# A slot's score steps in two visits to the row halves of the PE array, weight pieces behind the softmax, and another spread of the first groups

## The chip, the core and the metric

The kernel runs on one core of a Trainium2 chip. PE is TensorE, DVE is VectorE, ACT is ScalarE, POOL is GpSimd, SP issues the transfers; PEld is PE's loading of weights. The metric is the device time of one launch in microseconds, the median of three runs.

## The reference

Block-causal attention feeds a gated feed-forward with a spatial mix. Eight batches, eight heads, 576 positions, 64 dimensions a head, float32:

```python
scores = (q @ k.T) / 8                     # 576 x 576 per head, rows see blocks of 64 up to their own
attn   = softmax(scores)                   # with + 1e-9 in the divisor
x      = (attn @ v), heads side by side    # 576 x 512 per batch
h      = gelu(x @ w_in)                    # 576 x 1024, halves u and v
v_n    = (v - mean) / sqrt(var + 1e-6) * g_ln
v_s    = w_sg @ v_n + b_sg                 # over the 576 positions
out    = x + (u * v_s) @ w_out
```

`w_in` and `w_out` arrive as doubles.

## The kernel before

**Slots.** The attention of a pair of heads is a slot: 32 slots, four to a batch, n from 0. In slot n the kernel finishes pair n (transposes of the probabilities, products with the values, normalising) and makes scores and softmax of pair n+1. The rows of scores come in five tiles, 0 with 64 rows and 1 to 4 with 128; tile i reaches to column 64 + 128 i.

**Parts of the PE array.** Three kinds of matmul follow each other in a slot. Transposes of whole blocks (`pa`, `pb`, `pc`, `pe`, written `turn0`, `turn2`, `turn1`, `turn_sums`) and the feed-forward's groups use the whole array, 128 rows by 128 columns. Scores (`s`, steps 1 to 4) and the half blocks on the diagonal (`turn2_rest`, `turn1_rest`, `turn_first`) use its row halves, 64 rows. The products with the values (`ob`, `av0`, `av2`, `av1`, `av00`) use its column halves, 64 columns, one per head.

**Softmax.** A step writes its scores to two PSUM banks, one per head. DVE's `maximum` moves them to `prob` and keeps the negated maximum `negm`; tile 4 needs step1 and step2. ACT's `exponent` follows, and its sums go to `sums`. Then the next slot transposes `prob` into `pa`, `pb`, `pc`, and ACT and DVE copy these to `pt`.

**Groups.** The feed-forward of a batch runs in the holes of later slots: `hole(k)` issues k groups, one PSUM accumulation each. Of a batch there are 5 groups v, 8 u, 8 s, 8 o, and o stands behind the next batch's u. In steady state a slot n with n%4 = 0 has the v groups and two of u, n%4 = 1 the other u groups and one o, n%4 = 2 seven o, n%4 = 3 eight s. `PLAN` says how many groups go into each hole; `FIRST` says it for slots 4 to 7, the first that have any. When the v or u groups of a batch are done, ACT runs their GELU, with a table load before and after; layer norm and splitting into high and low parts follow on DVE, ACT and POOL (`run_side`).

**PSUM.** Five banks, tag "s", serve scores, groups and `ob`; `ob` is held from `av0` to the end of the slot. Three banks, tag "p", serve the transposes in turn, so a slot's second `pb` takes the bank of its first `pa`.

**Weights.** They are loaded and split in pieces, drawn by `weight_step`. A piece of `w_in` or `w_out` (128 x 256 doubles) costs a scaling on ACT, one tensor_scalar and two scalar_tensor_tensor on DVE, a cast on ACT and a subtraction on POOL. There are 16 pieces of `w_in`, 8 of `w_out`, 5 of `w_sg` and the gains. `WS` says how many steps a slot draws, `load_share` spreads them over four places; two are drawn before slot 0.

**What sets the order.** PE issues in program order (`PIN = "P"`). The other engines are ordered by a scheduler at build time, with its own picture of time, and may pull an instruction ahead of others of the program; `tc.issue_after` names an instruction that has to be issued before.

Of the kernel before, what the change touches and what calls it, by code (L numbers as in the profile page):

```python
# [28 lines left out]
def kernel(  # L29
# [73 lines left out]
    V, A, G, SP = Pinned(nc.vector, "V"), Pinned(nc.scalar, "A"), Pinned(nc.gpsimd, "G"), Pinned(nc.sync, "S")  # L103
# [116 lines left out]
    def load_weight(src, cols, dh, dl):  # L220

        W, AHEAD = 256, 4
        parts = [(c, slice(f, f + W)) for f in range(cols.start, cols.stop, W) for c in range(NC)]
        raws = {}

        def fetch(k):
            if k < len(parts):
                c, fs = parts[k]
                raws[k] = page(src.dtype, W, "raw")
                SP.dma_start(raws[k], src[c * P : (c + 1) * P, fs])  # L230

        for k in range(AHEAD):
            fetch(k)
        for k, (c, fs) in enumerate(parts):
            args = (raws.pop(k), dh[:, c, fs], dl[:, c, fs])
            if src.dtype == F32:
                split_weight(*args)
            else:
                from_f64(*args)
            fetch(k + AHEAD)  # L240
            yield True

    def load_spatial():
        for j in range(NT - 1):
            t = page(F32, S, "w")
            SP.dma_start(t, w_sgT[j * P : (j + 1) * P, :])
            split_weight(t, ws_h[:, j, :], ws_l[:, j, :])
            yield True

        j = NT - 1  # L250
        t = page(F32, S, "w")
        for hf in (0, 1):
            SP.dma_start(t[hf * BLK : (hf + 1) * BLK, :], w_sgT[j * P : S, :])
        t2 = page(F32, S, "w")
        G.memset(t2[BLK:, :], 0.0)
        SP.dma_start(t2[BLK : BLK + 1, :], b_sg.unsqueeze(0))
        SP.dma_start(t2[96:97, :], b_sg.unsqueeze(0))
        A.copy(ws_h[:, j, :], t)
        G.tensor_tensor(
            ws_l[:BLK, j, :], t[:BLK, :], ws_h[:BLK, j, :].bitcast(F32), op=ALU.subtract  # L260
        )
        A.copy(ws_l[BLK:, j, :], t2[BLK:, :])
        V.tensor_tensor(
            ws_l[96:97, j, :], t2[96:97, :], ws_l[96:97, j, :].bitcast(F32), op=ALU.subtract
        )
        yield True

    def load_gains():
        SP.dma_start(g_bc, g_ln.unsqueeze(0).broadcast_to([P, DH]))
        t = page(F32, S, "w")  # L270
        G.memset(t[BLK:, :DH], 1.0)
        V.tensor_copy(vone[BLK:, :], t[BLK:, :DH])
        yield True

    weights = deque(
        [
            ("v", load_weight(w_in, slice(DH, DFF), wi_h, wi_l)),
            ("v", load_gains()),
            ("u0", load_weight(w_in, slice(0, DH // 2), wi_h, wi_l)),
            ("u2", load_weight(w_in, slice(DH // 2, DH), wi_h, wi_l)),  # L280
            ("s", load_spatial()),
            ("o", load_weight(w_out, slice(0, DM), wo_h, wo_l)),
        ]
    )

    def weight_step():

        while weights and next(weights[0][1], None) is None:
            weights.popleft()

    def need(part):

# [3 lines left out]

    spill = {}
    xs = {}

    class Scores:  # L300

# [32 lines left out]
        def maximum(self, a, i, lo, hi):  # L334

            r, e = slice(0, QN[i]), EXT[i]
            m = self.negm[a][r, i : i + 1]
            V.tensor_tensor_reduce(
                self.prob[a][i][r, lo:hi],
                self.where[a, i, lo],  # L340
                mask[r, MW - (hi - lo) :] if 0 < i and hi == e else mask[r, : hi - lo],
                -0.125,
                3.0e38 if lo == 0 else m,
                op0=ALU.add,
                op1=ALU.min,
                accum_out=m,
            )

        def exponent(self, a, i):
            r, e = slice(0, QN[i]), EXT[i]  # L350
            A.activation(
                self.prob[a][i][r, :e],
                self.prob[a][i][r, :e],
                AF.Exp,
                bias=self.negm[a][r, i : i + 1],
                scale=-1.0,
                accum_out=self.sm[r, i, a : a + 1],
            )
# [153 lines left out]
    def run_side(k):  # L512

        while k > 0 and side and side[0][0] != "G":
            k -= 1
            side.popleft()[1]()
# [201 lines left out]
    def hole(k=1):  # L718

        while k > 0 and work:  # L720
            try:
                next(work[0])
                k -= 1
            except StopIteration:
                work.popleft()
# [3 lines left out]
    def load_share(n, k):  # L729

        if n < len(WS):
            for _ in range(WS[n] * (k + 1) // 4 - WS[n] * k // 4):
                weight_step()

    PLAN = ["1111111", "1111111", "1111111", "1111112"]

    FIRST = ["1111111", "1111110", "0000011", "1111110"]

    def slot(n, sc):
        va = Values(n, sc)  # L740
        nx = Scores(n + 1) if n + 1 < N else None
        g = [int(x) for x in (FIRST if n // 4 == 1 else PLAN)[n % 4]]
        if n + 2 < N:
            load_qk(n + 2)
        if n + 1 < N:
            load_v(n + 1)
        va.inverse()
        va.turn0(0)
        va.turn0(1)
        hole(g[0])  # L750
        load_share(n, 0)
        run_side(2)

        if nx:
            nx.step1()
        va.av0()
        if nx:
            nx.exponents(1)
        va.turn2()
        hole(g[1])  # L760
        run_side(2)
        va.turn2_rest()
        if nx:
            nx.step2()
        load_share(n, 1)
        hole(g[2])
        if nx:
            nx.exponents(4)
        run_side(2)
        va.turn1()  # L770
        va.turn1_rest()
        va.turn_first()
        if nx:
            nx.step3()
        va.av2()
        hole(g[3])
        load_share(n, 2)
        run_side(2)
        if nx:
            nx.exponents(3, 0)  # L780
            nx.step4()
        va.av1()
        va.av00()
        va.turn_sums()
        if nx:
            nx.exponents(2)
        hole(g[4])
        va.normalise()

        wait = n // (H // 2) > 0 and n % (H // 2) < 2  # L790
        pending.append(va.split)
        if not wait:
            while pending:
                pending.popleft()()
        run_side(2)
        if n + 2 < N:
            split_qk(n + 2)
        load_share(n, 3)
        hole(g[5])
        run_gelu()  # L800
        run_side(3)
        hole(g[6])
        run_side(3)
        if n % (H // 2) == 1:
            while pending:
                pending.popleft()()
        return nx
# [75 lines left out]
```

## Time and profile before

| | us |
|---|---|
| runs, median of three (lowest, highest) | 804.05 (802.69, 805.39) |
| profiled execution | 805.21 |
| its span | 803.1 |
| PE busy in it | 774.1 (96%) |
| DVE, ACT, POOL busy | 488.6, 452.4, 273.9 |
| slots 0 to 3 | 9.5 to 82.9 |
| slots 4 to 7 | 82.9 to 172.6 |
| slots 8 to 31 | 172.6 to 733.7 |
| groups behind the last slot | 733.7 to 803.1 |

A slot's start is read off PE's order of time: the first transpose into `pa`. In that view a row has start, length, engine, line, operation, tiles and count, and in brackets the idle time before it with what ended it. Lengths of matmuls overlap, so what one costs is the distance of two starts. The views by stretch give each engine's busy time between two times, and the granted clock as a share of full speed. A line of the source is nearly always that of a helper (L88 matmul, L91 transpose, L101 all other engines), so tiles' names tell rows apart; buffer numbers are left out.

### The profile page before, as it was taken

Reading aid. Unit: us, or ns where it says so; the run is one execution under the profiler, and the core shown is the slowest. Engines: PE = TensorE matmul, PEld = TensorE weight load, DVE = VectorE, ACT = ScalarE, POOL = GpSimd, SP = SyncE. Lnnn points to the kernel's source line nnn. Section 1 sums busy time; section 2 is a strip of 40 time slices with the busy share of each in tenths; the row PEclk is TensorE's granted clock in tenths of the full one; section 3 lists DMA queues with packets and bytes.
Section 4 is the critical chain, followed back from the end, with each engine's and each line's share of the span. In section 5 each row is a group of like instructions: output and inputs, shape, how many; then the busy total and the mean of one; then the engine's idle time right before and its main releaser. Section 6 shows DMA issues by size and latency. Waiting matters only on the chain.

```text
span 803.1 us, 15777 instructions
## 1 busy us (share of the span) xinstructions
PE 774.1 (96%) x5926; PEld 642.1 (80%) x5926; DVE 488.6 (61%) x1457; ACT 452.4 (56%) x1172; POOL 273.9 (34%) x331
## 2 busy tenths in 40 slices
PE   7579998999999999999999999999999999999998
PEld 5355686888888888897888888888888978888998
DVE  6955468884865567563765648655675637743532
ACT  5846569656864368435783368642694457821600
POOL 4773235651233314350233412333143402322111
PEclk8878998999999999999999999999999999999999
DMA  7522124212041123310242120321234102320042
GB/s 235 165 75 89 60 89 139 86 61 74 31 144 52 58 75 93 130 60 1 74 133 90 60 75 20 120 87 58 75 90 134 60 1 75 104 75 30 1 118 74
DMA packets 46911, 65.66 MB, mean 82 GB/s; under 512 B 4082, under 2 KB 22514, under 8 KB 46836
## 3 DMA queue, kind: packets, MB, share of 16 engines
q1 hardware_dynamic: 46836, 64.67, 25.1%
q8 instruction: 46, 0.75, 0.4%
q14 instruction: 29, 0.24, 0.1%
HBM read 45.78 MB, written 18.87 MB: 81 GB/s over the span
## 4 chain that ended last, share of the span: by engine, by line
PE 83%; ACT 0%; DVE 0%; issue 0%
PE accs L88 15%; PE acco L88 13%; PE accv L88 12%; PE accu L88 11%; PE ob L88 10%; PE s L88 9%; PE pb L91 4%; PE pc L91 3%; PE pa L91 3%; PE pe L91 1%; PE pd L91 1%; PE pd L88 0%; ACT pt L101 0%; DVE xr L101 0%; ACT w L101 0%
## 5 line engine op out<-in xcount | busy, mean ns | idle before, releaser
L101 ACT ACTIVATE prob<-prob,negm 128x448 f32<-128x448 f32 (+4 forms) x320 | 177.5, 557 | 107.3 <-DVE negm L101 104.6
L101 POOL TENSOR_TENSOR qk_l<-qk_f,qk_h 128x576 fp32r<-128x576 f32 x62 | 89.3, 1461 | 270.3 <-PE pe L91 114.0
L101 DVE CUSTOM_DVE_ANT_0 prob<-s,mask 128x288 f32<-128x288 f32 (+2 forms) x320 | 119.2, 422 | 78.9 <-PE s L88 77.4
L88 PE MATMUL ob<-pt,v_f 128*64 128x512 f32 (+4 forms) x640 | 111.7, 455 | 2.5 <-ACT pt L101 2.5
L101 POOL TENSOR_TENSOR gl<-u,gh 128x288 fp32r<-128x288 f32 x64 | 52.0, 818 | 114.1 <-DVE gh L101 89.1
L88 PE MATMUL s<-qk_h 64*128 64x288 f32 (+1 forms) x372 | 83.2, 353 | 0.0
L88 PE MATMUL accs<-ws_h,vh 128*128 128x288 f32 x256 | 78.6, 307 | 0.0
L88 PE MATMUL accu<-xh,wi_h 128*128 128x288 f32 x256 | 78.6, 307 | 0.0
L88 PE MATMUL acco<-gh,wo_h 128*128 128x288 f32 x256 | 78.2, 305 | 0.0
L88 PE MATMUL accu<-xl,wi_h 128*128 128x288 f32 x256 | 75.5, 295 | 0.0
L88 PE MATMUL accs<-ws_h,vl 128*128 128x288 f32 x256 | 75.5, 295 | 0.0
L88 PE MATMUL accs<-ws_l,vh 128*128 128x288 f32 x256 | 75.5, 295 | 0.0
L88 PE MATMUL accu<-xh,wi_l 128*128 128x288 f32 x256 | 75.5, 295 | 0.0
L88 PE MATMUL acco<-gh,wo_l 128*128 128x288 f32 x256 | 75.4, 294 | 0.0
L88 PE MATMUL acco<-gl,wo_h 128*128 128x288 f32 x256 | 75.4, 294 | 0.0
L88 PE MATMUL s<-qk_l,qk_h 64*128 64x288 f32 (+1 forms) x372 | 70.1, 297 | 0.9 <-POOL qk_l L101 0.9
L88 PEld LDWEIGHTS ob<-pt,v_f 128*64 128x64 f32 x640 | 38.9, 139 | 38.6 <-issue 21.6
L88 PE MATMUL s<-qk_h,qk_l 64*128 64x288 f32 (+1 forms) x372 | 65.5, 297 | 1.9 <-POOL qk_l L101 1.9
L88 PE MATMUL accv<-wi_h,xh 128*128 128x512 f32 x160 | 66.1, 413 | 0.0
L101 DVE TENSOR_TENSOR u<-accs,u 128x288 f32<-128x288 f32 x64 | 29.1, 454 | 56.1 <-PE accs L88 56.1
L88 PE MATMUL accv<-wi_l,xh 128*128 128x512 f32 x160 | 63.0, 393 | 0.0
L101 DVE TENSOR_TENSOR xr<-acco,xr 128x288 f32<-128x288 f32 x64 | 29.1, 455 | 54.9 <-PE acco L88 46.3
(104 smaller groups left out, 1948.9 us busy)
## 6 DMA issues: line engine op xcount, KB each, us to landing
spill<-x SPq DMA_DIRECT2D x32, 288.0 KB, 2.1
xr<-spill SPq DMA_DIRECT2D x32, 288.0 KB, 3.1
out_T<-xr SPq DMA_DIRECT2D x32, 288.0 KB, 2.9
qk_f<-in_qT SPq DMA_DIRECT2D x31, 288.0 KB, 2.9
qk_f<-in_kT SPq DMA_DIRECT2D x31, 288.0 KB, 3.4
v_f<-in_v SPq DMA_DIRECT2D x32, 256.0 KB, 3.0
raw<-in_w_in SPq DMA_DIRECT2D x16, 256.0 KB, 4.9
raw<-in_w_out SPq DMA_DIRECT2D x8, 256.0 KB, 3.0
```

Source lines behind the costliest of these rows:

```text
L88: return pin(nc.tensor.matmul(*a, **k), "P")
L91: return pin(nc.tensor.transpose(out, in_, identity), "P")
L101: return lambda *a, **k: pin(f(*a, **k), self.letter)
```

## The change

Inside a slot, `turn2` and `turn2_rest` move up behind the first hole, and step1 and step2 follow them directly; `av0` comes after both, and the exponents of tiles 1 and 4 after it. The second hole and the third now have nothing between them but a load share and `run_side`. Step4 moves up behind step3, ahead of `av2`, and the exponents of tiles 3, 0 and 2 stand together behind `av2`. Counted on PE, the array's part changes eight times in a slot and not eleven.

`newest` keeps the latest maximum and the latest exponent that the program has issued, and `weight_step` makes everything of a piece wait in the order for both. `FIRST` has 7, 6, 4 and 4 groups in slots 4 to 7, where it had 7, 6, 2 and 6.

```diff
     def weight_step():
 
-        while weights and next(weights[0][1], None) is None:
-            weights.popleft()
+        with ExitStack() as stack:
+            for ins in newest.values():
+                stack.enter_context(tc.issue_after(ins.ins))
+            while weights and next(weights[0][1], None) is None:
+                weights.popleft()
...
-            V.tensor_tensor_reduce(
+            newest["V"] = V.tensor_tensor_reduce(
...
-            A.activation(
+            newest["A"] = A.activation(
...
-    FIRST = ["1111111", "1111110", "0000011", "1111110"]
+    FIRST = ["1111111", "1111101", "0011011", "1011010"]
...
         run_side(2)
 
+        va.turn2()
+        va.turn2_rest()
         if nx:
             nx.step1()
+            nx.step2()
         va.av0()
         if nx:
-            nx.exponents(1)
-        va.turn2()
+            nx.exponents(1, 4)
         hole(g[1])
+        load_share(n, 1)
         run_side(2)
-        va.turn2_rest()
-        if nx:
-            nx.step2()
-        load_share(n, 1)
         hole(g[2])
-        if nx:
-            nx.exponents(4)
         run_side(2)
         va.turn1()
         va.turn1_rest()
         va.turn_first()
         if nx:
             nx.step3()
+            nx.step4()
         va.av2()
+        if nx:
+            nx.exponents(3, 0, 2)
         hole(g[3])
         load_share(n, 2)
         run_side(2)
-        if nx:
-            nx.exponents(3, 0)
-            nx.step4()
         va.av1()
         va.av00()
         va.turn_sums()
-        if nx:
-            nx.exponents(2)
         hole(g[4])
         va.normalise()
```

How it moves instructions, at three places; a row is line, operation, tiles and size. First PE in a slot with o groups, from the end of its first group; `acco` is the group, `s` scores, `ob` the products with the values, `pb` the transposes of turn2. Before:

```order
L88 MATMUL acco<-gh,wo_l 128x288
L88 MATMUL s<-qk_h 128x288 x2
L88 MATMUL s<-qk_l,qk_h 128x288 x2
L88 MATMUL s<-qk_h,qk_l 128x288 x2
L88 MATMUL s<-qk_h 128x192 x2
L88 MATMUL s<-qk_l,qk_h 128x192 x2
L88 MATMUL s<-qk_h,qk_l 128x192 x2
L88 MATMUL ob<-pt,v_f_103 64x512 x2
L91 MATMUL pb<-ident,prob_4_116 128x128
L91 MATMUL pb<-ident,prob_3_114 128x128
```

And in the change, from the end of turn2's whole blocks on:

```order
L91 MATMUL pb<-ident,prob_4_125 128x128
L91 MATMUL pb<-ident,prob_2_112 128x64
L91 MATMUL pb<-ident,prob_3_114 128x64
L91 MATMUL pb<-ident,prob_2_121 128x64
L91 MATMUL pb<-ident,prob_3_123 128x64
L88 MATMUL s<-qk_h 128x288 x2
L88 MATMUL s<-qk_l,qk_h 128x288 x2
L88 MATMUL s<-qk_h,qk_l 128x288 x2
L88 MATMUL s<-qk_h 128x192 x2
L88 MATMUL s<-qk_l,qk_h 128x192 x2
```

The half blocks of `pb` and both steps that make tile 4 now stand in a row, and `ob` comes after them. Second DVE in slot 0, up to the maxima of the next pair's first step (the ISA rows; `w` and `raw` are weight pieces). Before:

```order
L101 SCALAR_TENSOR_TENSOR w<-raw,w 128x256
L101 TENSOR_SCALAR w<-raw 128x256
L101 SCALAR_TENSOR_TENSOR w<-w 128x256
L101 SCALAR_TENSOR_TENSOR w<-raw,w 128x256
L101 TENSOR_SCALAR w<-raw 128x256
L101 ISA prob_4_134,negm<-s,mask 128x288
L101 ISA negm 128x1
L101 ISA prob_1_128,negm<-s,mask 128x192
L101 ISA negm 128x1
L101 SCALAR_TENSOR_TENSOR w<-w 128x256
```

And in the change:

```order
L101 COPY pt<-pa 128x512
L101 SCALAR_TENSOR_TENSOR w<-raw,w 128x256
L101 SCALAR_TENSOR_TENSOR w<-w 128x256
L101 COPY pt<-pb 128x512
L101 ISA prob_4_134,negm<-s,mask 128x288
L101 ISA negm 128x1
L101 ISA prob_1_128,negm<-s,mask 128x192
L101 ISA negm 128x1
```

The pieces that stood ahead of the maxima are gone to later places, and the copy of `pb` stands ahead of them instead. Third DVE in a slot with u groups, where layer norm (BN_STATS, BN_AGGR) of the batch runs. Before:

```order
L101 COPY pt<-pa 128x512
L101 SCALAR_TENSOR_TENSOR vv<-vv,stats,g_bc 128x512 x2
L101 BN_AGGR stats<-bs 128x2
L101 BN_STATS bs<-vv 64x6
L101 ISA prob_4_116,negm<-s,mask 128x288
L101 ISA negm 128x1
L101 ISA prob_1_110,negm<-s,mask 128x192
```

And in the change:

```order
L101 COPY pt<-pa 128x512
L101 SCALAR_TENSOR_TENSOR vv<-vv,stats,g_bc 128x512 x2
L101 BN_AGGR stats<-bs 128x2
L101 BN_STATS bs<-vv 64x6
L101 COPY pt<-pb 128x512
L101 BN_AGGR stats<-bs 64x2
L101 ISA prob_4_116,negm<-s,mask 128x288
L101 ISA negm 128x1
L101 ISA prob_1_110,negm<-s,mask 128x192
```

Here too the copy of `pb`, and one BN_AGGR, come ahead of the maxima.

More of the change, by code (lines that the diff above doesn't have):

```diff
@@ L298 @@
     xs = {}
+    newest = {}
     class Scores:
```

## The prediction

> **What bounds the kernel now.** I read the busy times by stretch first, cut at the first transposes of a slot (slots 0, 1, 3, 4, 5, 6, 7, and four later slots), then PE's order of time inside a slot, then what VectorE (DVE) and ScalarE (ACT) did while PE waited. The columns are length, then busy time (and instructions) of PE, PEld, DVE, ACT, POOL, the granted clock, DMA share and GB/s.
>
> ```profile
> 9.50:33.90 24.40, 16.98 (x96) 10.58 (x96) 23.02 (x74) 18.58 (x55) 13.74 (x15) 0.72 0.57 191
> 33.90:55.90 22.00, 14.06 (x97) 8.67 (x96) 13.40 (x49) 13.52 (x42) 16.55 (x17) 0.77 0.28 92
> 69.40:82.90 13.50, 11.98 (x98) 7.66 (x97) 8.47 (x32) 8.57 (x30) 5.34 (x6) 0.87 0.27 89
> 82.90:111.10 28.20, 26.69 (x178) 20.29 (x176) 11.84 (x38) 15.83 (x43) 8.90 (x10) 1.00 0.26 83
> 111.10:130.80 19.70, 19.70 (x169) 16.65 (x167) 16.68 (x47) 17.54 (x45) 5.51 (x6) 1.00 0.20 65
> 130.80:151.30 20.50, 16.80 (x126) 11.98 (x125) 18.96 (x53) 18.12 (x47) 14.45 (x16) 0.83 0.46 147
> 151.30:172.60 21.30, 21.30 (x182) 18.25 (x180) 18.20 (x52) 10.66 (x32) 12.05 (x15) 1.00 0.19 62
> 267.00:360.90 93.90, 93.90 (x743) 78.95 (x742) 57.49 (x173) 54.51 (x140) 30.28 (x35) 1.00 0.24 77
> ```
>
> So there are two regimes. From slot 7 on PE never rests, and only what PE itself does counts; whatever makes it wait is a loss of full size. In slots 0 to 3 no group of the feed-forward fills the slots, and the softmax loop sets the pace: PE, DVE, ACT, PE. Slots 2 and 3 take 13.5 us, slots 0 and 1 take 24.4 and 22.0. The next rows show what lies between, on PE and DVE in slot 0: the scores are there at 15.9, their maximum starts at 20.71, behind a row of weights' pieces.
>
> ```profile
> 15.52 0.41 PE L88 MATMUL s<-qk_h,qk_l 64*128 64x192 f32 x2
> ...
> 20.71 0.44 DVE L101 CUSTOM_DVE_ANT_0 prob<-s,mask 128x288 f32<-128x288 f32 x1
> ```
>
> **The change, term 1: slots 0 to 3.** I measure the loop at E, the end of a slot's last exponent (tile 2, second head). ACT's rows give E before slot 0, E of slots 0 and 2, and slot 3's tile 4, tile 3 and last exponent, with PE's wait in slot 3 among them; then the grouped rows price a weight piece, and a DVE row shows the product that frees a bank.
>
> ```profile
> 12.60 0.55 ACT L101 ACTIVATE prob<-prob,negm 128x320 f32<-128x320 f32 x1
> 39.76 0.56 ACT L101 ACTIVATE prob<-prob,negm 128x320 f32<-128x320 f32 x1
> 69.96 0.56 ACT L101 ACTIVATE prob<-prob,negm 128x320 f32<-128x320 f32 x1
> 71.72 0.66 PE L91 MATMUL pa<-ident,prob 128*128 128x128 f32 x4 [1.17 <-ACT pt L101]
> 78.28 0.78 ACT L101 ACTIVATE prob<-prob,negm 128x576 f32<-128x576 f32 x1 [0.64 <-DVE negm L101]
> 80.91 0.68 ACT L101 ACTIVATE prob<-prob,negm 128x448 f32<-128x448 f32 x1
> 83.43 0.55 ACT L101 ACTIVATE prob<-prob,negm 128x320 f32<-128x320 f32 x1
> ...
> L101 ACT ACTIVATE w<-raw 128x256 f32<-128x256 f32 x24 | 10.1, 433 | 6.3 <-issue 5.0 <-ACT w L101 1.0 <-DMA raw<-in_w_in 0.3
> L101 DVE SCALAR_TENSOR_TENSOR w<-raw,w 128x256 uint32<-128x256 uint32 x24 | 12.8, 535 | 0.1
> ...
> 84.58 0.69 DVE L101 TENSOR_TENSOR x<-pe,x 128x512 f32<-128x512 f32 x1
> ```
>
> E runs from 13.15 to 83.98: 70.8 us for four slots, 27.2 of it in slot 0. Afterwards slots 0 to 2 hold two pieces each and slot 3 the gains alone, and DVE's order puts each piece behind all maxima issued before it. A slot then goes like this from E. The second half of turn0 waits for the bank of x<-pe (85.27 in the row, E+1.3); with one weight scaling of 0.43 ahead of it, E+1.7. Four transposes of 0.11, turn2 and its rest 1.0, step1 0.67, step2 0.4: E+4.2 with the edges. DVE copies pt (0.68), takes the maxima of step1 (two of 0.45, two of 0.35) and the first of step2 (0.5): E+5.7, where before tile 4's exponent began at E+7.8 (78.28, E then 70.5). From there ACT is the path: two exponents of tile 4 of 0.87, one scaling 0.35, two copies of 0.53, 0.15, a cast of 0.3, and the six exponents of tiles 3, 0 and 2, which took 3.1 (80.91 to 83.98): E+12.4. Slot 3 lost 13% of its clock; I add 0.8 for that, 13.2 in all, and 13.6 for slot 0, whose PE starts at half clock. Four slots: 13.6 + 3 x 13.2 = 53.2, a gain of **17.6**. Bounds: 21 if the clock stays full (4 x 12.4); nothing if each piece puts its scaling, three DVE steps and cast, some 2.3, on the path and the earlier step2 gives nothing (13.45 + 2 x 2.3 = 18 a slot). I take a value near the first, for DVE and ACT were busy 8.5 of 13.5 in slot 3 and two pieces add under 3 to either. The removed cover is named: what hid the pieces was slot 0's stall itself; they now lie in slots 0 to 7.
>
> By the Trainium skill ("TensorE: Matmul & The Clock Gate", Part 1) the clock halves after an idle window of about 3.4 us; with waits of 2 us here that would not happen and term 1 would be 20. The trace does not bear it out: the longest wait in slot 3 was 1.17 and it yet had 0.87 of the clock.
>
> **Term 2: slots 4 to 7.** Sixteen of the 24 double-width pieces now run from slot 4 on. In slot 4 three pieces stand ahead of DVE's product and ACT's copy of x: some 1.25 later, less 0.56 for the changes of part (below): 28.9. Slot 5 has the bank waits of term 3 plus one cast of 0.55: 20.9. Slot 6 is the open one.
>
> ```profile
> 132.75 1.28 ACT L101 ACT_TABLE_LOAD   x1
> 133.48 0.40 PE L88 MATMUL s<-qk_h,qk_l 64*128 64x288 f32 x2 [1.13 <-POOL qk_l L101]
> 136.72 1.12 PE L88 MATMUL ob<-pt,v_f 128*64 128x512 f32 x1 [2.53 <-ACT pt L101]
> ```
>
> Its two waits came to 3.66, the lower clock to some 2.9. With turn2 now directly behind turn0 and no group between, turn2's second bank waits for ACT's copy of pa, which stands behind the table load and three GELUs: from S+1.1 (S its first transpose) to S+4.05, 3.0. Two more groups of 14 matmuls are 3.7: 9.6 of its own work + 7.4 + 3.0 + 1.5 for the clock = 21.5. Slot 7 gives those two groups up: 21.3 - 3.7 - 0.56 + 0.4 = 17.4. Together 88.7 against 89.7, a gain of **1.0**; bounds a gain of 5 (no wait in slot 6, none in slot 5) and a loss of 4 (the pieces push ACT in slots 4 and 6).
>
> **Term 3: slots 8 to 31.** First what a change of the array's part costs, on PE in slot 14.
>
> ```profile
> 316.77 0.29 PE L88 MATMUL acco<-gl,wo_h 128*128 128x288 f32 x1
> 316.90 0.29 PE L88 MATMUL acco<-gh,wo_l 128*128 128x288 f32 x1
> 317.13 0.40 PE L88 MATMUL s<-qk_h 64*128 64x288 f32 x2
> 317.37 0.30 PE L88 MATMUL s<-qk_l,qk_h 64*128 64x288 f32 x2
> 317.50 0.30 PE L88 MATMUL s<-qk_h,qk_l 64*128 64x288 f32 x2
> ...
> 317.72 0.28 PE L88 MATMUL s<-qk_l,qk_h 64*128 64x192 f32 x2
> 317.83 0.28 PE L88 MATMUL s<-qk_h,qk_l 64*128 64x192 f32 x2
> 318.03 1.08 PE L88 MATMUL ob<-pt,v_f 128*64 128x512 f32 x4
> ...
> 322.05 0.29 PE L88 MATMUL s<-qk_h,qk_l 64*128 64x288 f32 x1
> 322.26 0.40 PE L88 MATMUL acco<-gh,wo_h 128*128 128x288 f32 x1
> 322.50 0.30 PE L88 MATMUL acco<-gl,wo_h 128*128 128x288 f32 x1
> ```
>
> Start to start, a matmul of 288 columns takes 0.13. Whole array to row halves: 0.23 to the next start and 0.24 for the first pair, 0.21 more. Row halves to whole: 0.21 and 0.24, 0.19 more. Row halves to column halves: 0.20 against 0.11, and the first pair of ob some 0.05 slower, 0.14. Before, a slot has four changes into row halves, three from these to column halves, three from there to the whole, and one from row halves to the whole; after it has two, two, three, none, and one from the whole to column halves, which I price at 0.14 like its neighbour. 2 x 0.21 + 0.14 + 0.19 - 0.14, less 0.05 because a group and not a transpose follows av0: 0.56 a slot. Slot 31 has no next scores and gets 0.2: 23 x 0.56 + 0.2 = 13.1.
>
> What eats it: step1 and step2 now take four of the five banks "s" in a row and ob the fifth, so the group behind av0 waits until DVE has read step1's first bank. In a slot with u groups (n%4 = 1) DVE is late. Rows of slot 13, PE's first and DVE's:
>
> ```profile
> 293.25 1.03 PE L91 MATMUL pa<-ident,prob 128*128 128x128 f32 x8
> ...
> 295.84 0.67 DVE L101 COPY pt<-pa 128x512 f32<-128x512 f32 x1
> ...
> 297.84 0.65 DVE L101 BATCH_NORM_STATS2 bs<-vv 64x6 f32<-64x512 f32 x1
> 298.42 0.43 DVE L101 CUSTOM_DVE_ANT_0 prob<-s,mask 128x288 f32<-128x288 f32 x1
> ```
>
> DVE is free at +5.2 from the slot's start; now the copy of pb comes first (0.6), then the two maxima of that bank: +6.6. PE wants it at +5.7 (turn0 0.8, a group 1.7, turn2 0.65, edges 0.2, the rest with step2 0.75, step1 0.67, av0 1.0). A wait of **0.9**. Further on in that slot step4's second bank waits for ACT's copy of the second u group, behind the vn_t and vone scalings: +12.0 against +11.8, **0.25**. In a slot with o groups (n%4 = 2) turn2's second bank waits for pt<-pa, which ACT reaches only behind four GELUs:
>
> ```profile
> 314.56 1.03 PE L91 MATMUL pa<-ident,prob 128*128 128x128 f32 x8
> 317.21 0.57 ACT L101 COPY pt<-pa 128x512 f32<-128x512 f32 x1
> ```
>
> It ends at +3.2, turn2 wants it at +2.8: **0.45**. In v and s slots I find DVE 0.5 ahead. Six times 1.6 is 9.7, so term 3 is a gain of **3.4**; bounds a gain of 13.1 (no wait) and a loss of 8 (0.9 in every slot: 23 x 0.9 = 21). The banks' waits are read from ends of real rows, so I take them as they stand.
>
> The groups behind slot 31 (from 733.7) are untouched. **Sum:** 17.6 + 1.0 + 3.4 = 22.0 off the profiled execution's 805.21 (span 803.1 and 2.1 around it) is 783.2; the median of the runs, 804.05, lies 1.2 below that execution, so the median should read **782**.
>
> **The rivals.**
> *Banks come free in time* (term 3 is 12 instead of 3.4): speaks for it that DVE and ACT are busy 57 and 55 of 93.9 us; against it the row at 298.42. 773.
> *Banks are late in every slot*: the group behind av0 waits 0.9 in all 24 slots, term 3 a loss of 8: 793. For it, five of five banks are held; against it, DVE waited for PE in the o and s slots. The Trainium skill ("TensorEngine Tiling (Array Packing)", Gotcha 1: PSUM Pressure) says that row tiling raises the pressure on the banks; that is this case.
> *The clock stays full in slots 1 to 3* (term 1 is 20): 780.
> *Slower*: the sixteen late pieces and not the softmax come onto the path. Place: ACT and DVE in slots 4 to 7, where slot 6 already had 18 to 19 busy of 20.5. Price 2.3 each, 37 in all, against 22 won; it decides above 1.4 a piece. All at full price: 805.2 + 15 - 1.2 = 819. Against it: slot 4 leaves ACT 12 and DVE 16 us free.
> *It doesn't do what it says*: the pieces run early all the same and the changes cost nothing: 803. The order on DVE and the rows above speak against it.
>
> **The numbers.** Chances: forecast 55%, banks in time 14%, banks late 11%, full clock 10%, slower 7%, no effect 3%. About 0.3%, 2.4 us, is what a measurement of this kernel can tell from no change. Only the last two are not faster by that much: faster 0.91, within 0.03, slower 0.06. The forecast's own range is 775 to 789; with the two bank cases the range is 769 to 795, which leaves out the last two and some of the edges.
>
> **What would show it.** Slot 4's first transpose near 65 us instead of 82.9; DVE below 14 us busy in slot 0; in the late slots v and s shorter by 0.56, o by 0.1, u longer by 0.6, so four of them 93.3; a wait of PE on DVE (negm) behind av0 in u slots and on ACT (pt) at pb in o slots. Wrong would be: slots 0 to 3 above 15 each (pieces on the path), waits of PE at accu or accv for weights in slots 4 and 5, or a clock of half speed in slot 6 for more than 7 us.

## The result and the profile after

The changed kernel takes **792.94 us** (median of four runs, 792.58 to 793.08) against 803.92 (802.69 to 805.39) for the kernel before, taken beside it: a ratio of **0.9854, with a 95% interval of 0.9835 to 0.9872**. It is faster by 11 us, where 22 were forecast. The time lies inside the range of the prediction (769 to 795), near its upper end, and beside the number of the rival "banks late in every slot" (793), so the number alone does not say which reason holds. The profile does. Of all the runs below one, of `only_pieces`, took 4007 us and is left out of that kernel's ratio.

Busy time by stretch, cut at the first transposes of a slot: slots 0 to 7, then a batch of four steady slots. Columns as in the prediction: length, busy time of PE, PEld, DVE, ACT, POOL, granted clock, DMA share, GB/s.

```profile
10.57:25.90 15.33, 12.41 (x97) 8.74 (x96) 12.96 (x51) 11.84 (x38) 5.99 (x7) 0.89 0.39 132
25.90:40.85 14.95, 11.54 (x97) 8.25 (x96) 13.06 (x39) 10.23 (x34) 6.87 (x8) 0.89 0.26 81
40.85:56.70 15.85, 12.87 (x98) 8.74 (x97) 13.00 (x40) 10.54 (x34) 7.38 (x9) 0.78 0.29 92
56.70:70.90 14.20, 11.46 (x98) 7.97 (x97) 11.18 (x36) 9.38 (x30) 6.30 (x7) 0.88 0.42 140
70.90:106.00 35.10, 29.14 (x177) 22.30 (x176) 23.16 (x63) 22.21 (x60) 18.87 (x21) 0.90 0.41 126
106.00:127.00 21.00, 19.88 (x170) 16.66 (x169) 18.05 (x47) 18.78 (x47) 9.79 (x10) 1.00 0.18 54
127.00:148.20 21.20, 17.78 (x154) 14.35 (x152) 20.68 (x53) 16.72 (x42) 12.24 (x13) 1.00 0.39 130
148.20:166.30 18.10, 17.23 (x153) 14.34 (x151) 15.62 (x49) 9.77 (x30) 9.82 (x12) 1.00 0.25 72
259.40:352.30 92.90, 92.18 (x742) 78.57 (x741) 56.96 (x173) 54.40 (x140) 30.50 (x35) 1.00 0.25 78
```

Slots 0 and 1 are no longer 24 and 22 us long. But slots 2 and 3, which held no pieces and took 13.5 each, are now longer (15.8 and 14.2), and slot 4 went from 28.2 to 35.1. A batch is 1.0 us shorter. The profiled spans, 803.1 and 791.0, divide so:

| part | before | forecast | after | won |
|---|---|---|---|---|
| start of slot 0 | 9.5 | | 10.6 | -1.1 |
| slots 0 to 3, first transpose to first transpose | 73.4 | | 60.3 | 13.1 |
| the same from E to E (term 1) | 70.8 | 53.2 | 57.3 | 13.5 (forecast 17.6) |
| slots 4 to 7 (term 2) | 89.7 | 88.7 | 95.5 | -5.8 (forecast 1.0) |
| slots 8 to 31 (term 3) | | | | 5.9 (forecast 3.4) |

The two rows on slots 0 to 3 measure the same thing at different marks; the first of them, with the rows around it, gives the 12.1 of the spans. The start of slot 0 is not the change: over the fourteen profiles of this study it lies between 9.4 and 10.7, and two kernels whose source differs from slot 4 on alone had 9.60 and 10.57, with the same order of PE's, DVE's and ACT's instructions ahead of it.

**The head of a slot.** The forecast lost its time between E, the end of the last exponent, and tile 4's exponent. Rows of ACT in slot 2: the two last exponents before E, the copies behind them, tile 4's first exponent and the last exponent of the slot.

```profile
41.53 0.55 ACT L101 ACTIVATE prob<-prob,negm 128x320 f32<-128x320 f32 x1
42.08 0.42 ACT L101 ACTIVATE w<-raw 128x256 f32<-128x256 f32 x1
42.40 0.56 ACT L101 COPY x<-ob 128x512 f32<-128x512 f32 x1
...
50.60 0.76 ACT L101 ACTIVATE prob<-prob,negm 128x576 f32<-128x576 f32 x1
...
56.82 0.55 ACT L101 ACTIVATE prob<-prob,negm 128x320 f32<-128x320 f32 x1
```

E is 42.08, tile 4 begins at E+8.5 where the forecast had E+5.7, and from there to the next E (57.37) it takes 6.8, the forecast's 6.7. So in slot 2 the head alone was 2.8 too short; over the four slots the heads took 7.0, 8.2, 8.5 and 7.9 and the rest of the slot 6.3, 6.3, 6.8 and 6.3. DVE in that head, and behind it the row of POOL that lies beside it:

```profile
40.94 0.28 DVE L101 TENSOR_SCALAR w<-raw 128x256 uint32<-128x256 uint32 x1
41.25 1.58 DVE L101 SCALAR_TENSOR_TENSOR w<-raw,w 128x256 uint32<-128x256 uint32 x1
42.76 1.36 DVE L101 TENSOR_TENSOR ri<-sums,tiny 128x10 f32<-128x10 f32 x1
44.15 0.22 DVE L101 RECIPROCAL ri<-ri 128x10 f32<-128x10 f32 x1
44.29 0.36 DVE L101 SCALAR_TENSOR_TENSOR w<-w 128x256 uint32<-128x256 uint32 x1
44.56 0.69 DVE L101 TENSOR_TENSOR x<-pe,x 128x512 f32<-128x512 f32 x1
...
41.15 2.95 POOL L101 TENSOR_TENSOR qk_l<-qk_f,qk_h 128x576 fp32r<-128x576 f32 x2 [1.23 <-PE pe L91]
```

None of these rows of DVE shows a wait. A step of a weight piece that takes 0.41 elsewhere took 1.58, and a sum over ten columns took 1.36. POOL makes its two subtractions for qk_l in just that time, 41.15 to 44.10. x<-pe, which frees the bank for the second half of turn0, ends at E+3.2 where the forecast had E+1.7. That is 1.5 of the 2.8. The other 1.3 lies behind x: from there to tile 4's exponent it takes 5.3, where the forecast had 4.0, and in all this time PE's granted clock was 0.50 (window from the end of x<-pe to tile 4's exponent):

```profile
45.25:50.60 5.35, 5.29 (x32) 3.96 (x32) 4.14 (x15) 1.59 (x6) 2.36 (x3) 0.50 0.66 213
```

**Slot 4.** Rows of DVE, POOL and PE at its head:

```profile
71.25 3.02 DVE L101 TENSOR_SCALAR w<-raw 128x256 uint32<-128x256 uint32 x3
74.19 0.75 DVE L101 SCALAR_TENSOR_TENSOR w<-raw,w 128x256 uint32<-128x256 uint32 x2
...
76.35 0.68 DVE L101 TENSOR_TENSOR x<-pe,x 128x512 f32<-128x512 f32 x1
...
76.99 2.30 POOL L101 TENSOR_TENSOR wi_l<-w,wi_h 128x256 fp32r<-128x256 f32 x3
79.25 0.31 POOL L101 TENSOR_TENSOR xh<-x,xh 128x64 fp32r<-128x64 f32 x1
...
73.74 0.66 PE L91 MATMUL pa<-ident,prob 128*128 128x128 f32 x4 [2.13 <-ACT pt L101]
...
79.62 0.80 PE L88 MATMUL accv<-wi_h,xh 128*128 128x512 f32 x1 [3.83 <-POOL xh L101]
```

Three pieces stand ahead of x on DVE from 71.25 to 76.35, so that x<-pe ends at 77.03, which is E+5.5 (E is 71.58), where the forecast had some E+2.6; then the three wi_l stand ahead of xh on POOL. The first v group needs all four x of the batch, so it waits 3.83 in its middle, and PE waits 6.0 in all. Behind that wait PE ran close to half clock:

```profile
79.60:86.40 6.80, 6.78 (x35) 4.71 (x35) 3.79 (x15) 2.70 (x7) 1.33 (x1) 0.54 0.63 222
```

**The late slots** went as forecast in kind: v, s and o slots are shorter by 0.47, 0.44 and 0.44 (26.24 to 25.77, 25.00 to 24.56, 21.31 to 20.87), u slots longer by 0.39 (21.31 to 21.70). The wait that was forecast for u slots is there. From PE's waits over the whole run (total us, times, longest):

```profile
PE accu L88 <- DVE negm L101: 5.1, 7, 0.7
```

### The profile page after: what moved, and what is told of

The parts are those of the page before. It is cut to its first block, busy times and chain, and to the rows that moved or that the text cites. A ratio compares the mean times of both kernels' runs of the same rounds, so it can differ in the third digit from the quotient of the medians.

```text
span 791.0 us, 15794 instructions
## 1 busy us (share of the span) xinstructions
PE 757.9 (96%) x5926; PEld 640.4 (81%) x5926; DVE 495.5 (63%) x1457; ACT 450.6 (57%) x1172; POOL 272.4 (34%) x331
## 4 chain that ended last, share of the span: by engine, by line
PE 77%; DVE 12%; ACT 8%; issue 1%; SPq 1%; DMA 1%; POOL 1%; DVEq 0%; POOLq 0%; ACTq 0%
PE accs L88 14%; PE acco L88 13%; PE accv L88 13%; PE ob L88 9%; PE s L88 8%; PE accu L88 8%; PE pc L91 3%; PE pb L91 3%; DVE bs L101 3%; ACT prob L101 3%; PE pa L91 2%; DVE w L101 2%; ACT L101 1%; DVE prob L101 1%; PE pe L91 1%; DVE pt L101 1%
## 5 line engine op out<-in xcount | busy, mean ns | idle before, releaser
L101 POOL TENSOR_TENSOR qk_l<-qk_f,qk_h 128x576 fp32r<-128x576 f32 x62 | 91.9, 1502 | 231.6 <-issue 98.9
L101 DVE CUSTOM_DVE_ANT_0 prob<-s,mask 128x288 f32<-128x288 f32 (+2 forms) x320 | 117.0, 421 | 64.6 <-PE s L88 64.6
L88 PE MATMUL ob<-pt,v_f 128*64 128x512 f32 (+4 forms) x640 | 105.7, 443 | 0.9 <-ACT pt L101 0.8
L88 PE MATMUL s<-qk_h 64*128 64x288 f32 (+1 forms) x372 | 87.4, 341 | 0.4 <-ACT u L101 0.4
L88 PE MATMUL s<-qk_l,qk_h 64*128 64x288 f32 (+1 forms) x372 | 82.2, 302 | 0.0
L88 PE MATMUL s<-qk_h,qk_l 64*128 64x288 f32 (+1 forms) x372 | 77.9, 299 | 0.0
L88 PEld LDWEIGHTS s<-qk_h 64*128 64x128 f32 x372 | 64.0, 188 | 1.4 <-ACT u L101 0.6
L88 PEld LDWEIGHTS s<-qk_h,qk_l 64*128 64x128 f32 x372 | 63.8, 187 | 0.0
```

Of the source, the lines that this page charges most:

```text
L88: return pin(nc.tensor.matmul(*a, **k), "P")
L101: return lambda *a, **k: pin(f(*a, **k), self.letter)
```

## Experiments

### The order and the queue apart

`old_pieces` is the changed kernel with the pieces free to run early again; `only_pieces` is the kernel before with the queue alone.

```diff
 # old_pieces, in weight_step
-        with ExitStack() as stack:
-            for ins in newest.values():
-                stack.enter_context(tc.issue_after(ins.ins))
-            while weights and next(weights[0][1], None) is None:
-                weights.popleft()
+        while weights and next(weights[0][1], None) is None:
+            weights.popleft()
 # only_pieces: the reverse of this, in the kernel before
```

> The changed kernel, with the weights' pieces free to run as early as before: the new order of step1 to step4 and the groups 7-6-4-4 alone. Theory (the prediction's terms stand apart): slots 0 and 1 stall again behind pieces, 24 and 22 us long, slots 2 and 3 near 13; slot 4 begins near 83 as before and is 28 long; batches of four slots from slot 8 on keep their 92.9. Time near 797, of which 5.9 less than before comes from slots 8 to 31. Rival (the new order is what shortens slots 0 to 3, the queue does little): slot 4 begins near 73, time near 791.

> The kernel before, with the pieces queued behind the newest maximum and the newest exponent and nothing else changed. Theory: slots 0 to 3 are near 15 to 16 each, slot 4 begins near 72 and is some 34 long, since the three pieces at its head stand ahead of x there as well; batches from slot 8 on stay 93.9; time near 798. Rival (the queue works only together with the early step2): slots 0 to 3 above 17 each, slot 4 begins after 78, time 803 or more.

Measured: `old_pieces` 791.97 (ratio to before 0.9852, 0.9814 to 0.9889), `only_pieces` 803.5 (0.9991, 0.9978 to 1.0004). **The new order, with the new groups of slots 4 to 7, gives the whole gain, and the queue gives nothing.** The theory missed both numbers. The rival had the time of `old_pieces` right (791), though not its slots: slot 4 begins at 79.6, not 73. For `only_pieces` too the rival had the time (803), but the slots went nearly as the theory had them: slot 4 begins at 74.3 and is 35.7 long. Slot lengths from the traces:

| | slots 0, 1, 2, 3 | their sum | slot 4 | slots 5 to 7 | batch |
|---|---|---|---|---|---|
| before | 24.5, 22.0, 13.5, 13.5 | 73.4 | 28.2 | 61.5 | 93.9 |
| only_pieces | 16.1, 14.7, 16.2, 16.8 | 63.9 | 35.7 | 61.3 | 93.9 |
| old_pieces | 20.8, 27.5, 10.4, 11.2 | 69.9 | 27.7 | 59.3 | 92.9 |
| changed | 15.3, 14.9, 15.8, 14.2 | 60.3 | 35.2 | 60.3 | 92.9 |

The two edits add almost exactly. The queue wins 9.5 in slots 0 to 3 in either order, and loses 7.5 in slot 4 in both; the rest goes in slots 5 to 7 and in the start. The order with the groups wins 3.5 and 3.6 in slots 0 to 3, 0.5 in slot 4, 1 to 2 in slots 5 to 7 and 5.9 from slot 8 on.

Why slots 2 and 3 matter shows in `old_pieces`, where they hold no pieces (windows of slots 1 to 4):

```profile
30.50:58.00 27.50, 16.91 (x98) 11.41 (x97) 25.32 (x57) 16.38 (x50) 19.58 (x20) 0.69 0.33 105
58.00:68.40 10.40, 9.53 (x97) 6.96 (x96) 8.33 (x32) 7.64 (x26) 3.35 (x5) 1.00 0.35 114
68.40:79.60 11.20, 9.78 (x97) 6.96 (x96) 8.40 (x32) 8.45 (x29) 5.37 (x6) 1.00 0.35 107
79.60:107.30 27.70, 26.29 (x177) 20.35 (x176) 11.14 (x38) 15.77 (x43) 8.93 (x10) 1.00 0.31 98
```

Slot 2's 10.4 is short because its first transpose came late, behind slot 1's pieces. From E to E both slots take 11.2 (E at 58.3, 69.5 and 80.6), against 13.5 in the old order: the early step2 wins 2.3 a slot. The forecast's 12.4 holds 0.43 + 0.35 + 0.3, some 1.1, for a slot's pieces, so without pieces it is 11.3: the loop itself was forecast right. From tile 4's exponent to the end of the last one ACT works without a gap, 5.7; the forecast's 6.7 less 0.65 for pieces is 6.0. Rows of `old_pieces` on ACT in slot 3:

```profile
74.95 0.76 ACT L101 ACTIVATE prob<-prob,negm 128x576 f32<-128x576 f32 x1
...
80.09 0.55 ACT L101 ACTIVATE prob<-prob,negm 128x320 f32<-128x320 f32 x1
```

With 11.2 for a slot without pieces, the pieces' prices follow; they are taken from E to E, since slot 0's first transpose lies 3.7 ahead of its E and that of a slot without pieces 1.0. In `old_pieces` slots 0 and 1 hold sixteen of the double-width pieces (counted by their first step on DVE: 12 and 4) and take 44.8, which is 22.4 more than two empty slots: 1.4 each. In the changed kernel slots 0 to 2 hold eight (3, 2, 3) and slot 4 the other eight. Slots 0 to 3 take 57.3, 12.5 more than four empty ones, **1.6 a piece** with the lost clock in it; slot 4 pays 7.5, 0.9 a piece. Of these 7.5, 4.6 are longer waits of PE and 2.9 longer busy time, at a granted clock of 0.90 instead of 1.00 (the windows of slot 4 in both). So the sixteen cost 20.0 spread and 22.4 bunched; slots 5 to 7 (1.0 longer), the start of slot 0 (0.8 later) and the change of mark at slot 4 (0.4) take those 2.4 back but for 0.2. The last eight lie in slots 6 to 8 in all four kernels.

### What holds up the head

Four runs take away what stands ahead of x. `behind_x` lets a piece queue also behind DVE's cast of x:

```diff
-            V.tensor_copy(hi[:, :S], x)
+            newest["V"] = V.tensor_copy(hi[:, :S], x)
```

> The changed kernel, in which a piece also queues behind DVE's cast of x to xh of the slot before, so that no piece stands ahead of x<-pe, xh and the second half of turn0. Theory (the loss of slot 4 is the place of three pieces, 71.25 to 76.35 on DVE, not their work): slot 4 goes from 35.2 to about 29, slots 1 to 3 lose about 0.5 each; time near 786. Rival (sixteen late pieces cost their work wherever they stand): slot 4 stays within 1 of 35, or slots 5 to 7 grow by what it wins; time 791 to 794.

Measured: 786.1 (0.9780, 0.9762 to 0.9798), the theory's number. Slot 4 is 31.2 (29 expected), slots 1 to 3 are 13.9, 13.9 and 13.7, and slot 5 gave 1.2 back. So 4.0 of slot 4's 7.5 came from the place of the pieces and not from their work. Slots 1 to 3 won 3.6 together, where 1.5 was expected.

`ql_on_dve` takes POOL's two subtractions out of the head:

```diff
-            G.tensor_tensor(lo[:, i, :], t[:, i, :], hi[:, i, :].bitcast(F32), op=ALU.subtract)
+            (V if n < 6 else G).tensor_tensor(
+                lo[:, i, :], t[:, i, :], hi[:, i, :].bitcast(F32), op=ALU.subtract
+            )
```

> The changed kernel, in which the subtraction that makes qk_l runs on DVE instead of POOL for the first slots (the products of slots 2 to 5). Theory (DVE instructions that read two SBUF operands or cast stand still while POOL's two subtractions of 1.5 us run): the stretched rows go (ri<-sums from 1.36 to 0.16, w<-raw,w from 1.58 to 0.41 in slot 2), DVE pays two subtractions of about 0.65 instead, slots 1 to 3 are shorter by 0.5 to 1.2 each and slot 4 by 1 to 2; time 788 to 791. Rival (DVE has simply too much to do, 13.0 busy of 15.0 in slot 1): 1.3 more on DVE in each of four slots, time 796 to 798.

Measured: 785.87 (0.9777, 0.9759 to 0.9794), more than the theory asked and 10 us from the rival. DVE has *more* to do and the slots are shorter: 12.2, 13.6, 13.6. DVE's groups in slots 1 to 3 of the changed kernel, columns busy us, mean ns:

```profile
L101 DVE SCALAR_TENSOR_TENSOR w<-raw,w 128x256 uint32<-128x256 uint32 x5 | 4.4, 889 | 0.2
L101 DVE TENSOR_TENSOR ri<-sums,tiny 128x10 f32<-128x10 f32 x3 | 3.8, 1255 | 0.3 <-ACT prob L101 0.3
L101 DVE SCALAR_TENSOR_TENSOR w<-w 128x256 uint32<-128x256 uint32 x5 | 3.0, 605 | 1.8 <-ACT w L101 1.8
```

The same groups of `ql_on_dve`, slots 1 to 3:

```profile
L101 DVE SCALAR_TENSOR_TENSOR w<-w 128x256 uint32<-128x256 uint32 x5 | 2.1, 426 | 1.9 <-ACT w L101 1.8
L101 DVE SCALAR_TENSOR_TENSOR w<-raw,w 128x256 uint32<-128x256 uint32 x5 | 2.1, 416 | 0.1
L101 DVE TENSOR_TENSOR ri<-sums,tiny 128x10 f32<-128x10 f32 x3 | 0.5, 154 | 0.0
```

889 to 416 ns, 605 to 426 and 1255 to 154: the stretch belongs to POOL's instructions. By the Trainium skill ("SBUF — State Buffer", Who interferes with whom) a VectorE instruction with two SBUF operands and a GpSimd instruction that reads SBUF exclude each other for the whole instruction, and so do single-operand VectorE instructions in their two-port mode; the rows agree, and x<-pe, with one operand from PSUM, keeps its 0.69 beside POOL's copy of rx. DVE saved 6.6 and paid 4.2 for its own subtractions (three times 1.41), 2.4 net; the slots won 5.5. The other 3 are waits and half-clock stretches of PE that went with it (the clock of slots 1 to 3 rose from 0.89, 0.78, 0.88 to 1.00, 0.88, 0.87); the runs do not part them. Slot 1, with two pieces and at full clock, shows what the forecast's loop is without the stretch: x<-pe ends at E+2.0 and tile 4's exponent begins at E+5.9 (forecast E+1.7 and E+5.7), and the slot takes 12.2, against the forecast's 12.4 at full clock (window of slot 1):

```profile
25.90:38.10 12.20, 9.83 (x97) 6.93 (x96) 11.13 (x41) 9.66 (x32) 3.94 (x6) 1.00 0.30 99
```

Two more runs: `clear_head` joins both and lets a piece queue on ACT behind the copies of x too; `ri_behind_x` leaves qk_l on POOL, but lets ri<-sums queue behind the product of x.

```diff
 # both, in normalise
-            copy("a", x[:, :BLK], self.o0)
+            newest["A"] = copy("a", x[:, :BLK], self.o0)
...
-            V.tensor_tensor(x[:, :BLK], self.t4[:, 128:192], x[:, :BLK], op=ALU.mult)
+            newest["V"] = newest["x"] = V.tensor_tensor(
+                x[:, :BLK], self.t4[:, 128:192], x[:, :BLK], op=ALU.mult
+            )
 # ri_behind_x, in inverse, around the sum
+            with ExitStack() as stack:
+                if "x" in newest:
+                    stack.enter_context(tc.issue_after(newest["x"].ins))
...
```

> The changed kernel with both remedies of the slots' heads: a piece queues behind x on ACT (its copy of pd) and on DVE (the product and the cast), and qk_l for the products of slots 2 to 5 is made on DVE. Theory (the two act on different stretches of the same head: the pieces' order 6.8, POOL's lock 7.1, of which some 2 are shared): slots 1 to 3 near 12 each, slot 4 near 29; time 779 to 782. Rival (they remove the same wait twice): 785 to 786.

> As the run with both remedies, but qk_l stays on POOL and DVE's ri<-sums, which stands still there for 1.2 us, queues behind the product of x instead. Theory (only what stands ahead of x on DVE matters): the head is as short as with qk_l on DVE, without DVE's 1.3 us for it: slots 1 to 3 near 12 each, time 779 to 782. Rival (the lock then holds up pt<-pa or the cast behind x, and with them turn2's bank): slots 1 to 3 above 13, time 783 to 786.

Measured: 784.14 (0.9745, 0.9728 to 0.9762) and 783.63 (0.9744, 0.9728 to 0.9761). The first comes out between theory and rival, the second at its rival's number. `behind_x` and `ql_on_dve` win 6.8 and 7.1 singly and 8.8 joined, so some 5 of it is won only once. In `ri_behind_x` the stretched step now stands behind x, but between the copies of pa and pb (DVE, slot 2):

```profile
42.57 0.62 DVE L101 COPY pt<-pa 128x512 f32<-128x512 f32 x1
43.11 1.27 DVE L101 SCALAR_TENSOR_TENSOR w<-raw,w 128x256 uint32<-128x256 uint32 x1
44.31 0.68 DVE L101 COPY pt<-pb 128x512 f32<-128x512 f32 x1
```

Its slots 1 to 3 ran at full clock throughout and took 13.4, 13.4 and 13.5 (windows of slots 1 to 3):

```profile
25.10:38.40 13.30, 10.76 (x97) 7.19 (x96) 10.68 (x39) 9.76 (x32) 7.07 (x8) 1.00 0.34 110
38.40:51.80 13.40, 10.87 (x97) 7.30 (x96) 10.77 (x39) 9.85 (x32) 7.08 (x8) 1.00 0.28 89
51.80:65.30 13.50, 11.14 (x97) 7.42 (x96) 10.86 (x36) 9.44 (x32) 7.59 (x9) 1.00 0.53 167
```

That is still 2.2 above a slot without pieces (11.2), at the same clock. So two pieces cost 1.1 each here with no clock lost, and 0.5 each in slot 1 of `ql_on_dve`, where POOL's subtractions are out of the way.

### The wait in u slots

`av0_late` moves av0 away from step2, so that ob is taken later:

```diff
-        va.av0()
         if nx:
             nx.exponents(1, 4)
...
+        va.av0()
         va.av2()
```

> The changed kernel with av0 moved from behind step2 to directly ahead of av2: ob is taken from the banks three groups later, seven changes of the array's part a slot instead of eight. Theory (the group behind av0 waits because step1, step2 and ob hold all five banks): the waits of PE at accu and accs for DVE (negm), 5.1 and 1.5 us in all, are gone, a u slot goes from 21.71 to about 20.8, the other slots lose 0.1 to 0.2 through the change that is saved; a batch goes from 92.9 to 91.4, time near 785. Rival (the wait only moves: now step3, step4 and ob hold the five banks and the group behind av2 waits for step3's maxima): PE waits for negm at the fourth group, a batch stays at 92.9 or more, time 792 to 796.

Measured: 790.1 (0.9821, 0.9806 to 0.9836). The wait at accu is gone (5.1 to 0.7 in all), and v, o and s slots, with one change of the array's part less, win 0.15, 0.16 and 0.13. But u slots went up from 21.70 to 22.85; PE's waits and a u slot's window:

```profile
PE ob L88 <- ACT pt L101: 13.9, 10, 2.0
...
PE accu L88 <- DVE negm L101: 0.7, 1, 0.7
...
185.40:208.20 22.80, 21.50 (x181) 18.45 (x179) 18.41 (x53) 18.70 (x47) 7.34 (x8) 1.00 0.15 43
```

The wait moved, though not where the rival had it: not to DVE's maxima but to ACT's copies of pt. That they come later because av0 now holds two of pt's four buffers longer is argued, not shown: no run gives pt a fifth buffer. The gain in the time came from slots 1 to 3 (12.9, 12.9, 12.4) and slot 4 (30.6), which the expectation had left out; slots 0 and 6 took 2.4 and 3.7 back.

`u_group_first` keeps av0 and puts the second group ahead of it in u slots only:

```diff
+        group_first = n >= 8 and n % 4 == 1
+        if not group_first:
+            va.av0()
-        va.av0()
         if nx:
             nx.exponents(1, 4)
         hole(g[1])
+        if group_first:
+            va.av0()
```

> The changed kernel, in which av0 stands behind the second group instead of ahead of it in the u slots from slot 8 on (n%4 = 1, six of them); nothing else moves. Theory (that group waits 0.72 for DVE because step1, step2 and ob hold the five banks): the wait at accu is gone, one change of the array's part more costs 0.1 to 0.2, a u slot goes from 21.71 to 21.1 to 21.2, time 789 to 790. Rival (the wait moves to av0, whose bank is then the one that DVE has not read, or to the third group): a u slot stays at 21.7 or more, time 793 or more.

Measured: 793.7 (0.9881, 0.9859 to 0.9904), and u slots at 21.70 as before the edit. The wait at accu is gone here as well, and a new one stands at the scores of step3 or step4, for ACT's copy of u:

```profile
PE s L88 <- ACT u L101: 2.5, 7, 0.4
...
PE accu L88 <- DVE negm L101: 0.7, 1, 0.7
```

The rival's number, by another wait. Of the 0.72 removed, 0.36 a slot came back there and 0.13 to 0.16 is the one change of part more; 0.2 is not accounted for. Neither way of removing this wait shortened a u slot: in a u slot the next one lies close behind it.

### The groups

```diff
-    FIRST = ["1111111", "1111101", "0011011", "1011010"]
+    FIRST = ["1111111", "1111110", "0000011", "1111110"]
```

> The changed kernel with the groups of slots 4 to 7 as before, 7-6-2-6 instead of 7-6-4-4. Theory (slot 6 has room for two more groups only because PE waits there on ScalarE and DVE): slot 6 falls from 21.2 by less than the two groups' 3.7, to about 19.5, and slot 7 takes them at full price, from 18.2 to 21.7; the four slots together are 1.5 to 2.5 longer, time 794 to 796. Rival (the split of the groups is neutral, for the late pieces fill slot 7's DVE instead): within 1 of 793.

Measured: 795.28 (0.9892, 0.9869 to 0.9914). Slot 6 is 18.6 and slot 7 is 23.2; slots 4 to 7 take 97.7 instead of 95.5. The theory holds: by the slots' lengths 7-6-4-4 is worth 2.2 here, because slot 6 waits anyway. The ratios alone would hardly tell it: their intervals touch.

### Versions that put it together

`head_and_av0` is `clear_head` with `av0_late`. `combined` is `ri_behind_x` with the group ahead of av0 in late u slots and av0 late in slots 2, 3, 4, 5, 7 and the other late slots; `combined_2` leaves u slots and slots 2, 5 and 6 as they were:

```diff
+        late = n in (3, 4) or (n >= 7 and n % 4 != 1)
+        if not late:
+            va.av0()
-        va.av0()
...
+        if late:
+            va.av0()
         va.av2()
```

> Both remedies of the heads (qk_l on DVE, pieces behind x on ACT and DVE) and av0 directly ahead of av2. Theory: the two gains add, since one lies in slots 0 to 4 and the other from slot 8 on: the time is that of both remedies less what the move of av0 gives alone, 771 to 775. Rival (av0's move lengthens slots 0 to 3, where the array is not full, by putting av0 behind the scores that ACT and DVE wait for or by holding pt's buffers): 776 to 780.

> The pieces and ri<-sums queued behind x, the group ahead of av0 in the u slots from slot 8 on, and av0 directly ahead of av2 in slots 2, 3, 4, 5, 7 and in the v, o and s slots from slot 8 on. Theory (each remedy was seen at its own place: 783.6 with the first; the second 0.6 times six; the third 0.15 in each of 18 slots and up to 3 in slot 4): 774 to 778. Rival (av0 ahead of av2 and the pieces behind x meet in slots 4 to 7, as they did when both remedies stood together, 789.3): 783 to 787.

> The pieces and ri<-sums queued behind x, and av0 directly ahead of av2 in slots 3, 4 and 7 and in the v, o and s slots from slot 8 on; the u slots, and slots 2, 5 and 6, keep av0 behind step2. Theory (in the first combination slot 2's 15.9 and slot 6's 24.4 came from av0's place in slots 2 and 5): slot 2 near 13.4, slot 6 near 21.5, slot 5 near 21.4, the rest as there; time 777 to 780. Rival (slot 6's wait for DVE's pt comes from the shorter slots ahead of it, not from av0): slot 6 stays above 23.5, time 780 to 783.

Measured, in this order: 789.27 (0.9815, 0.9801 to 0.9830), 781.23 (0.9721, 0.9700 to 0.9742; between its theory and its rival) and **779.81 (0.9710, 0.9694 to 0.9726)**, the fastest of all and faster than both kernels. The first lost 5 to `clear_head`: its six late u slots took 1.15 more each, which is `av0_late`'s own loss, and slots 0 to 3 another 2.7. In `combined_2` slot 2 is 13.3 and slot 6 is 21.5, as its theory had it. Its slots 1, 2 and 4 and a batch:

```profile
25.50:38.90 13.40, 10.85 (x98) 7.28 (x97) 10.77 (x39) 9.85 (x32) 7.06 (x8) 1.00 0.34 109
38.90:52.20 13.30, 10.76 (x97) 7.19 (x96) 10.68 (x39) 9.74 (x32) 7.07 (x8) 1.00 0.27 89
67.90:96.00 28.10, 25.91 (x178) 20.54 (x177) 21.48 (x63) 20.79 (x55) 16.89 (x19) 1.00 0.53 170
248.00:340.40 92.40, 91.68 (x741) 78.78 (x740) 54.48 (x173) 54.25 (x140) 30.64 (x34) 1.00 0.24 78
```

## Why the prediction was right, and where it was not

The sign and the range were right, and the two regimes are there. The forecast of 782 was 11 too low: it lost 4.1 in term 1 and 6.8 in term 2 and won 2.5 in term 3. The other 2.5 are the later start of slot 0, the change of mark at slot 4, and the 1.2 by which the forecast put the median below the profiled execution, where here the two agree.

**Term 1 (17.6 forecast, 13.5 measured).** The step that failed is the head of a slot, "with one weight scaling of 0.43 ahead of it, E+1.7" and the "E+5.7" built on it. E+1.7 was taken from rows where nothing stood beside x<-pe. With a piece and ri<-sums ahead of it on DVE, both stretched beside POOL's subtractions, x<-pe ended at E+3.2 in slot 2, and behind it PE ran at half clock, 5.3 instead of 4.0. The four heads took 8.8 more than 4 x 5.7 and the rest of the slots 1.0 less than 4 x 6.7; 3.6 had been put in for the clock, which leaves the 4.1. The other steps held: a slot without pieces takes 11.2 (11.3 by the forecast's own terms), and one with two pieces 12.2 where the clock was full and POOL did not stretch DVE (12.4). So 1.1 for a slot's pieces was right for their work alone; with the stretch and the lost clock a slot paid 3.1 in the mean. How these two share it is known for the head of slot 2 only. Had the pieces been free, term 1 would have been 26.0 (70.8 less 4 x 11.2). The bound "if each piece puts ... some 2.3 on the path" had too high a price (1.6) on too high a base (13.45 instead of 11.2).

What the prediction took as the cause, that pieces leave slots 0 and 1, is not where the gain is. Moving them won 9.5 there, lost 7.5 in slot 4 and left the time as it was, in either order; the early step2, the fewer changes of part and the new groups carry the whole of the 11. The time stayed inside the range in part by luck, since term 3 gave back 2.5 of what the other two missed.

**Term 2 (1.0 forecast, 5.8 lost).** Slots 5, 6 and 7 came out at 20.9, 21.2 and 18.2 against 20.9, 21.5 and 17.4. Slot 6 met its number partly by luck: its clock stayed at 1.00, so the 1.5 put in for the clock was not paid, and turn2's second bank waited 1.9 (for DVE's copy) instead of 3.0; waits of 1.5 elsewhere and 0.8 of work took their place. Slot 4 was 35.2 against 28.9. The failed step is "three pieces ... some 1.25 later": they stood on DVE for 5.1, of which 2.2 is the stretch of three TENSOR_SCALARs (3.02 instead of 0.84), and their POOL part then held up xh, which the step did not follow at all though it named DVE and ACT. The slower rival named this mechanism, late pieces on the path, and was to decide above 1.4 apiece. In slot 4 it came true, at 0.9 for each of eight pieces. But the other eight of its sixteen lay in slots 6 to 8 before the change as well, and with the 1.0 of slots 5 to 7 it is 0.5 apiece over the sixteen, too little to decide.

**Term 3 (3.4 forecast, 5.9 measured).** Right in kind. The eleven changes of part less three give 0.44 to 0.47, where 0.56 was summed from single rows; `av0_late` measures one change at 0.13 to 0.16. The wait behind av0 in u slots is 0.72 (0.9 forecast). The o slots' wait of 0.45 for pt<-pa did not come: in slot 10 that copy ends at 217.21, as forecast, but pb's whole blocks, from 216.49 on, run on at 0.11 each, the second pb's from 216.81. So there the second pb did not wait for the first pa's bank, as "PSUM" ahead of the prediction has it; why is not settled. Together: 3.4 + 4.6 (six times the 0.45 that did not come and the 0.31 by which a u slot's waits, 0.39 + 0.45 against 1.15, were smaller) - 2.5 (23 times 0.11 for the cheaper changes) = 5.5 of the 5.9.

**The rivals.** Banks in time: no, u slots wait. Banks late in every slot: no, only u slots do, so its 793 was met for other reasons; the pressure on the banks that the Trainium skill names ("TensorEngine Tiling (Array Packing)", Gotcha 1: PSUM Pressure) shows in one kind of slot of four. Full clock in slots 1 to 3: not in the changed kernel (0.89, 0.78, 0.88); what it would have brought depends on POOL. At full clock a slot with two pieces took 13.4 where DVE's steps were still stretched (`ri_behind_x`, `combined_2`), and 12.2, near that rival's 12.4, where they were not (slot 1 of `ql_on_dve`). No effect: no, although for the queue alone it is true.

**The signs.** Slot 4's first transpose came at 70.9 (near 65 forecast, 82.9 before), DVE in slot 0 was busy 13.0 (below 14), u slots waited at accu for negm. Of the signs that were to prove it wrong two appeared: slots 1 and 2 near or above 15, and a wait at accv in slot 4, though for xh and not for weights.

## What to carry to other kernels

Before work is moved out of a stall, price it at its new place: sixteen pieces cost 22.4 us bunched in a stall of their own and 20.0 spread into the heads of tight loops, so the move was worth nothing until they queued behind the instruction that frees the next bank. On VectorE, price an instruction by whether GpSimd is at work on SBUF at that moment, not by its mean; a ten-column sum can cost a whole GpSimd instruction. And test the parts of a change singly: here one of them, the queue, carried nothing of the gain.

## What the runs showed of the hardware

- DVE's instructions with two SBUF operands end with POOL's instruction: ri<-sums over 10 columns 1255 ns in the mean beside POOL's subtraction and 154 without it, w<-raw,w 889 against 416. TENSOR_SCALAR with one operand stood still as well (three in 3.02 us instead of 0.84).
- The moment of slot 0's first transpose varied between 9.4 and 10.7 us over fourteen profiles, with the same order of PE's, DVE's and ACT's instructions ahead of it.
- PE's granted clock can fall to half behind short waits: in the changed kernel it was 0.50 from 45.25 to 50.60, and no wait of PE in slots 0 to 3 was longer than 1.5 us. In `ri_behind_x` it stayed at 1.00 in slots 1 to 3, with waits of up to 1.3.
- A change of the array's part costs 0.13 to 0.16 us in this kernel, the mean over three saved at once and over one saved alone agreeing.
